# Attention followed by a four-expert layer on one core: a new table of order priorities, and other engines for the last output tiles

## The chip, the cores and the metric

The kernel runs on one core of a Trainium2 chip. The metric is the device time of one execution in microseconds (us), as the median of several runs of the same program. A core has one engine for matrix products (TensorE, PE below), whose weight loads are a row of their own (PEld), VectorE (DVE), ScalarE (ACT), GpSimd (POOL) and SyncE (SP), and 16 DMA engines that move data between the core's own memories and the chip's large one. Each engine runs its own list of instructions in order and waits on semaphores for the others. Products land in PSUM, which here is cut into eight banks of 128 x 512 numbers.

## The reference

Everything is fp32. First there is attention over 8 batches of 8 heads with 64 columns each, 512 local and 32 global positions. Then comes an attention in each of four experts, of which every position takes its best two.

```python
# attention: window = 32, scale = 1/sqrt(64)
s_g   = scale * q_g @ concat(k_g, k_l).T                # global queries see all
out_g = softmax(s_g) @ concat(v_g, v_l)
s_ll  = where(|i - j| <= window, scale * q_l @ k_l.T, -1e9)
s_lg  = scale * q_l @ k_g.T
out_l = softmax(concat(s_lg, s_ll)) @ concat(v_g, v_l)
x     = concat(out_g, out_l)        # turned to (batch, 544, 512)
# experts: 4 of 64 columns each
logits = x @ w_gate                 # top two, softmax over the two -> w
for e in range(4):
    q, k, v = x @ wq[e], x @ wk[e], x @ wv[e]
    a   = softmax(causal(scale * q @ k.T))
    out += w_e * (a @ v @ wo[e])    # only where e is one of the two
```

## The kernel before

**Work.** A pair is two heads of one batch, so there are 32 pairs, four to a batch. For a pair the local attention goes through `p1_load` and `p1_load_values` (loads of kn, qn and of the values v), `p1_trans` (PE turns kn and qn, L575), `p1_scores` (64 small products into two banks, L605), `p1_softmax` (DVE takes scores, mask and minimum out of PSUM, L617; ACT does exp, L620), `p1_ptrans` (PE turns the probabilities, tile st, L638), `p1_av` (64 small products with the values, L668) and `p1_turn` (PE turns the result xn, L638). POOL copies each pair's values into overlapping windows, nine copies a pair (L319: six v<-v, three v<-vg). Global queries have steps of their own (L732, L772). The loads of L335 are all issued by SP, but for the very first.

The experts' part of a batch has the projections `m_v` (L833) and `m_qk` (L802), each a product of high and low parts; the scores `m_scores` (L955, pairs of 512-column banks, two experts c = 0, 1 at a time and three sizes t); `m_softmax` (DVE L970, ACT L974, the normalisation L990 by POOL, or DVE for the last batch); the turn of the probabilities (tile pm, L638, copied out as ptl and ptu by L319 and L317); `m_av` (L1040); the same for the 32 tail positions of a batch (L1062, L1107); and the four output tiles of a batch, with a tail tile for every four batches (`out_tile`: six products L1126, one copy out of PSUM to tile ot, one to four DMAs L1133).

**Order.** The program runs through 42 steps; step s has the scores of pair s, the products with the values of pair s-2, and a quarter of the experts' work of a batch that began six steps before. Nothing is issued in this order, though. Each operation is recorded with an engine (or a choice, as "ACT|DVE"), an expected time in ns, and a priority of 100 times its step plus a small lateness; to this a table adds a number that depends on the operation's kind, its expected time and its step modulo 8:

```python
o.prio += SHIFT.get(kind, {}).get((round(ns[0]), int(self.prio // 100) % 8), 0)
```

One entry so moves all operations of that kind, time and step modulo 8, in all batches. Then `place` puts the operations in a row one at a time, on an assumed clock per engine. For PE it takes the smallest of

```python
f[0] + CHANGE * (f[1].shape != shape) + PULL * (f[1].prio - pe[0].prio)
```

(the time at which it could start, a price where the products divide the PE array otherwise than those before, and a price for low priority); other engines take the lowest priority among what could start soon. Eight PSUM banks, and two to four buffers of each other tile, are given out in the order of the row. So the table decides each engine's list of instructions, and which bank and which buffer is waited for.

**The last tiles.** `out_tile` copies its bank to ot by ACT. The DMA is issued by ACT for tiles 2, 3 and the tail tile, and by SP, as four DMAs, for tiles 0 and 1 (`MIRRORED`). The program ends with the four tiles of batch 7 and the second tail tile.

Of the kernel before, what the change touches and what calls it, by code (L numbers as in the profile page):

```python
# [49 lines left out]
class Op:  # L50
    def __init__(self, k, engs, ns, fn, prio, packets, shape, slow):
# [24 lines left out]
        "evac": {(276, 0): 110, (316, 2): -110, (369, 2): 110, (369, 6): 110, (448, 4): 30, (475, 0): 90, (475, 4):  # L76
        50, (475, 7): 80},
        "high_low": {(477, 3): 140, (477, 5): 100},
        "load": {(540, 1): 80, (540, 4): -150, (540, 7): -150},
        "m_av": {(2220, 1): -60, (2220, 3): -20, (2220, 7): -70},  # L80
        "m_gates": {(130, 7): -30, (350, 7): -110, (630, 6): 150, (648, 3): 150, (950, 7): -150},
        "m_qk": {(1504, 0): -40, (1504, 3): 60, (1504, 4): 40, (1504, 6): -150},
        "m_scores": {(431, 2): 100, (431, 6): 60, (722, 1): -30, (722, 3): 40, (722, 5): 100, (745, 2): -90, (745, 6):
        -20},
        "m_softmax": {(80, 1): -40, (80, 2): 100, (80, 6): -70, (211, 1): 40, (211, 3): 150, (211, 5): -130, (211, 7):
        -40, (386, 1): -150, (386, 7): -150, (431, 7): -50, (477, 1): -120, (477, 3): -100, (492, 4): 100, (492, 6):
        -80, (599, 7): -90, (610, 4): 20, (705, 2): 140},
        "m_tail_av": {(583, 1): -110, (583, 5): 30},
        "m_tail_scores": {(110, 7): -100, (610, 3): 10, (859, 7): -50},
        "m_v": {(1440, 2): -80, (1440, 5): 150},  # L90
        "m_v_tails": {(256, 3): 150},
        "out_tile": {(450, 1): 130, (1400, 1): -70, (1400, 5): 40},
# [12 lines left out]
        "setup": {(163, 2): -70},  # L105
        "turn_halves": {(250, 0): 60, (250, 1): -100, (250, 2): 100, (250, 5): -150, (312, 0): 30, (312, 2): -110,
        (312, 4): 70, (312, 6): -70, (374, 0): -150, (374, 2): -150, (374, 4): -100, (374, 6): 80, (499, 0): 40, (499,
        2): -90, (499, 3): 20, (499, 4): -90, (499, 7): 10},
        "turned": {(84, 1): 10, (84, 3): 50, (84, 5): 50, (84, 7): -70, (255, 5): 150},
}  # L110


class Plan:

    ENGINES = ("PE", "DVE", "ACT", "POOL", "SP")

    def __init__(self):
        self.ops = []  # L120
# [144 lines left out]
def fused_kernel(ctx: ExitStack, tc: tile.TileContext, q_l, k_l, v_l, q_g, k_g, v_g,  # L265
                 w_gate, wq, wk, wv, wo, out):
    nc = tc.nc
    B, H, SL, D = q_l.shape
# [15 lines left out]
    op = plan.op  # L284
# [1045 lines left out]
```

## Time and profile before

| | |
|---|---|
| three runs | 484.69, 485.98, 487.23 us; median 485.98 |
| profiled execution | 484.76 us, span 482.9 us |
| granted PE clock, mean | 0.992 of full speed |
| busy share of the span | PE 95%, PEld 83%, DVE 79%, ACT 67%, POOL 60% |
| instructions | 25126 |

The span runs from the first to the last recorded instruction; 1.9 us of the execution lie outside it. A busy share says how long an engine had an instruction in work, not that it went at its best pace. The profiled execution is 1.2 us below the median of the runs.

### The profile page before, as it was taken

The numbers are of one execution on the slowest core, as the hardware profiler recorded it, in microseconds if no ns is written. First come the engines' busy times: TensorE is split into PE (matmuls) and PEld (weight loads), VectorE is DVE, ScalarE is ACT, GpSimd is POOL, SyncE is SP. The second block draws the span as 40 slices with busy tenths as digits, with TensorE's granted clock in tenths as the row PEclk, the third lists the DMA queues.
The fourth block names the chain that finished last, engine by engine and source line by source line (L and its number), as shares of the span: only waits on it lengthen the run. The fifth ranks groups of instructions, "written<-read, shape, count | busy, mean of one in ns | idle before, by whom it ended". The sixth has DMA issues, their size and how long they took to land.

```text
span 482.9 us, 25126 instructions
## 1 busy us (share of the span) xinstructions
PE 460.3 (95%) x10252; PEld 400.0 (83%) x10252; DVE 380.9 (79%) x1684; ACT 324.4 (67%) x1171; POOL 291.4 (60%) x563
## 2 busy tenths in 40 slices
PE   8869998999999999999999999999999999999987
PEld 6657896888988988879889888879888899789865
DVE  7889589999985986779985977859986786557480
ACT  1867278797865785767955966847885674645472
POOL 8996988978585496809587296916859122311320
PEclk9899999999999999999999999999999999999999
DMA  9967666764355334444256234453022000200123
GB/s 189 199 126 154 123 119 115 150 106 83 67 103 125 68 56 95 111 79 87 41 108 148 50 54 79 104 122 77 3 56 89 4 3 3 70 21 2 27 65 109
DMA packets 182388, 40.96 MB, mean 85 GB/s; under 512 B 177664, under 2 KB 177664, under 8 KB 182272
## 3 DMA queue, kind: packets, MB, share of 16 engines
q1 hardware_dynamic: 172784, 32.96, 35.1%
q10 hardware_dynamic: 9488, 6.40, 4.8%
q8 instruction: 80, 1.31, 1.2%
q14 instruction: 36, 0.29, 0.2%
HBM read 30.42 MB, written 8.91 MB: 81 GB/s over the span
## 4 chain that ended last, share of the span: by engine, by line
PE 77%; DVE 9%; DMA 6%; SPq 2%; issue 2%; POOL 2%; ACT 0%; ACTq 0%; POOLq 0%; DVEq 0%
PE bank L802 15%; PE bank L1126 10%; PE bank L638 9%; PE bank L833 9%; PE bank L1040 7%; PE bank L955 6%; PE bank L605 5%; PE bank L668 5%; PE bank L732 2%; SPq L335 2%; PE bank L772 2%; DMA v<-in_v_l_dram 2%; DMA kn<-in_k_l_dram 2%; PE bank L1062 2%; DVE st L617 1%
## 5 line engine op out<-in xcount | busy, mean ns | idle before, releaser
L319 POOL COPY v<-v 32x512 f32<-32x512 f32 (+3 forms) x192 | 115.8, 604 | 17.8 <-DMA v<-in_v_l_dram 8.2
L990 POOL TENSOR_SCALAR pm<-pm,msm,gate 128x512 f32<-128x512 f32 (+3 forms) x124 | 74.3, 613 | 64.0 <-ACT pm L974 13.3
L620 ACT ACTIVATE st<-st,sm 128x128 f32<-128x128 f32 x256 | 99.6, 393 | 13.0 <-DVE sm L617 12.7
L319 POOL COPY v<-vg 32x640 f32<-32x640 f32 (+1 forms) x96 | 67.2, 702 | 33.5 <-PE bank L772 22.9
L974 ACT ACTIVATE pm<-pm,msm 128x512 f32<-128x512 f32 (+3 forms) x128 | 71.0, 557 | 20.8 <-DVE msm L970 20.7
L617 DVE CUSTOM_DVE_ANT_0 st<-bank,band 128x128 f32<-128x128 f32 x256 | 57.9, 281 | 2.7 <-PE bank L605 2.5
L620 ACT ACTIVATION_READ_ACCUMULATOR st<-st,sm 128x1 f32 x256 | 48.7, 190 | 0.0
L955 PE MATMUL bank<-kt,qt 64*32 64x32 f32 (+15 forms) x1024 | 41.3, 393 | 2.3 <-issue 1.5
L605 PE MATMUL bank<-kd,qp 64*32 64x128 f32 x2048 | 40.1, 276 | 1.4 <-issue 1.1
L317 ACT COPY ptu<-bank 128x384 f32<-128x384 f32 (+1 forms) x42 | 21.4, 543 | 27.6 <-PE bank L638 17.3
L802 PE MATMUL bank<-xh,wk_hi 128*128 128x272 f32 x128 | 38.7, 302 | 0.0
L970 DVE CUSTOM_DVE_ANT_0 pm<-bank,cmask 128x512 f32<-128x512 f32 (+1 forms) x64 | 37.5, 614 | 0.4 <-PE bank L955 0.3
L802 PE MATMUL bank<-xh,wq_hi 128*128 128x272 f32 x128 | 37.3, 292 | 0.0
L833 PE MATMUL bank<-wv_hi,xh 128*128 128x260 f32 x128 | 37.1, 290 | 0.0
L802 PE MATMUL bank<-xl,wk_hi 128*128 128x272 f32 x128 | 36.9, 288 | 0.0
L802 PE MATMUL bank<-xh,wq_lo 128*128 128x272 f32 x128 | 36.9, 289 | 0.0
L802 PE MATMUL bank<-xl,wq_hi 128*128 128x272 f32 x128 | 36.9, 288 | 0.0
L802 PE MATMUL bank<-xh,wk_lo 128*128 128x272 f32 x128 | 36.9, 288 | 0.0
L668 PE MATMUL bank<-v,ptw 128*32 128x64 f32 x2048 | 36.2, 223 | 0.1
L605 PEld LDWEIGHTS bank<-kd,qp 64*32 64x32 f32 x2048 | 32.3, 107 | 4.7 <-issue 2.3
L833 PE MATMUL bank<-wv_lo,xh 128*128 128x260 f32 x128 | 36.3, 283 | 0.0
L833 PE MATMUL bank<-wv_hi,xl 128*128 128x260 f32 x128 | 36.1, 282 | 0.0
(183 smaller groups left out, 1319.7 us busy)
## 6 DMA issues: line engine op xcount, KB each, us to landing
v<-in_v_l_dram SPq DMA_DIRECT2D x61, 120.0 KB, 3.4
kn<-in_k_l_dram SPq DMA_DIRECT2D x104, 64.0 KB, 2.5
qn<-in_q_l_dram SPq DMA_DIRECT2D x104, 64.0 KB, 2.6
out_dram<-ot SPq DMA_DIRECT2D x64, 64.0 KB, 1.7
out_dram<-ot ACTq DMA_DIRECT2D x16, 256.0 KB, 2.8
v<-in_v_l_dram SPq DMA_DIRECT2D x30, 64.0 KB, 3.4
kn<-in_k_l_dram SPq DMA_DIRECT2D x8, 128.0 KB, 3.7
qn<-in_q_l_dram SPq DMA_DIRECT2D x8, 128.0 KB, 4.4
```

Of the source, the lines that this page charges most:

```text
L319: ENG[e].tensor_copy(out, in_)
L605: nc.tensor.matmul(sp[h].t[32 * g:32 * g + 32, 128 * t:128 * t + 128], qp.t[rows, 32 * u:32 * u + 32], kd.t[rows, c:c + 128], start=True, ...
L617: op("DVE", 211, lambda e, h=h, t=t, i=i: nc.vector.tensor_tensor_reduce(out=st.t[:, h, t], in0=sp[h].t[:, 128 * t:128 * t + 128], in1=ban ...
L620: op("ACT", 385, lambda e, h=h, t=t, i=i: nc.scalar.activation(st.t[:, h, t], st.t[:, h, t], AF.Exp, bias=sm.t[:, 0, i:i + 1], scale=-1.0, ...
L638: nc.tensor.transpose(two[y].t[:, k, :], block()[rows], ident[rows, rows])
L668: nc.tensor.matmul(xq.t[32 * g:32 * g + 32, t, h, :], pt.t[:, h, 32 * u:32 * u + 32], v.t[:, h, window(u), :], start=True, stop=True)
L802: nc.tensor.matmul(pp.t, w[:, ch, cols], x(part, ch)[:, n], start=(ch == 0 and w is hi and part == 0), stop=(ch == NCH - 1 and part == 1))
L833: nc.tensor.matmul(pv.t, x(part, ch)[:, 128 * i:128 * i + 128], w[:, ch, :], start=(ch == 0 and part == 0 and w is hi), stop=(ch == NCH - ...
L955: nc.tensor.matmul(sp[x].t[32 * g:32 * g + 32, at:at + n], qt.t[rows, q0:q0 + 32], kt.t[rows, :n], start=True, stop=True)
L974: op("ACT", 280 + 0.83 * n, lambda e, x=x, at=at, n=n, s=s: nc.scalar.activation(pm.t[:, x, at:at + n], pm.t[:, x, at:at + n], AF.Exp, bia ...
L990: lambda e, x=x, at=at, n=n, row=row, s=s: ENG[e].tensor_scalar(pm.t[:, x, at:at + n], pm.t[:, x, at:at + n], sm.t[:, 3, s:s + 1], gate.t[ ...
L1126: nc.tensor.matmul(po.t, lhs(part, c), w[:, c, :], start=(c == 0 and part == 0 and w is hi), stop=(c == 1 and part == 1))
```

## The change

Two things change. The whole table SHIFT has other values, in the same form; the diff shows two lines of each table. And the output tiles of the last batch, with the second tail tile, may have their bank copied by ACT or DVE and their DMAs issued by SP or ACT, whichever `place` finds free, where both were fixed.

```diff
 SHIFT = {
-        "m_av": {(2220, 1): -60, (2220, 3): -20, (2220, 7): -70},
-        "m_qk": {(1504, 0): -40, (1504, 3): 60, (1504, 4): 40, (1504, 6): -150},
...
+        "m_av": {(1560, 1): 110, (2220, 1): 40, (2220, 3): -50},
+        "m_qk": {(1504, 4): 30, (1504, 7): -10},
...
-    def out_tile(y, lhs, dsts, via="ACT"):
+    def out_tile(y, lhs, dsts, via="ACT", last=False):
...
-        evac(lambda: ot.t, lambda: po.t, 512, [po], [ot], "ACT")
+        evac(lambda: ot.t, lambda: po.t, 512, [po], [ot], "ACT|DVE" if last else "ACT")
         for dst, rows in dsts:
-            op(via, 450, lambda e, dst=dst, rows=rows: ENG[e].dma_start(dst, ot.t[rows]), r=[ot], late=-10,
+            op("SP|ACT" if last else via, 450, lambda e, dst=dst, rows=rows: ENG[e].dma_start(dst, ot.t[rows]), r=[ot], late=-10,
...
-        out_tile(y, lambda part, c: M[b, "yo"][part].t[:, c, at:at + 128], dsts, "SP" if i in MIRRORED else "ACT")
+        out_tile(y, lambda part, c: M[b, "yo"][part].t[:, c, at:at + 128], dsts, "SP" if i in MIRRORED else "ACT",
+                 b == B - 1)
...
-                 [(out[4 * g + r, SL:, :], slice(32 * r, 32 * r + 32)) for r in range(4)])
+                 [(out[4 * g + r, SL:, :], slice(32 * r, 32 * r + 32)) for r in range(4)], last=4 * g + 4 == B)
```

The changed file is two lines shorter ahead of its functions, so L335 of before is L333 after, L668 is L666, and so on. Three places show what the table does.

SP's loads at the head of the program, before, from the 13th transfer on. A 128x4x64 tile of kn or qn is the load of one head of pairs 0 to 5 (32x16x32 stands for the later pairs, four a tile), v a piece of a pair's values, in_moe_ the experts' weights.

```order
L335 DMA kn<-in_k_l_dram 128x4x64 x2
L335 DMA qn<-in_q_l_dram 128x4x64 x2
L335 DMA pm<-in_moe_wv_dram 128x8x64 x2
L335 DMA msm<-in_moe_w_gate_dram 128x4x4
L335 DMA pm<-in_moe_wk_dram 128x8x64 x2
L335 DMA v<-in_v_l_dram 96x5x64 x2
L335 DMA v<-in_v_l_dram 128x2x64
L335 DMA v<-in_v_l_dram 96x5x64 x2
L335 DMA v<-in_v_l_dram 128x2x64
L335 DMA kn<-in_k_l_dram 128x4x64
```

The same stretch after:

```order
L333 DMA v<-in_v_l_dram 96x5x64 x2
L333 DMA v<-in_v_l_dram 128x2x64
L333 DMA kn<-in_k_l_dram 128x4x64 x4
L333 DMA qn<-in_q_l_dram 128x4x64 x4
L333 DMA pm<-in_moe_wv_dram 128x8x64 x2
L333 DMA msm<-in_moe_w_gate_dram 128x4x4
L333 DMA pm<-in_moe_wk_dram 128x8x64
L333 DMA pm<-in_moe_wq_dram 128x8x64 x2
L333 DMA pm<-in_moe_wk_dram 128x8x64
L333 DMA v<-in_v_l_dram 96x5x64 x3
L333 DMA vg<-in_v_g_dram 32x8x64
```

Pair 2's values (its first three pieces here) move ahead of the weights, all of kn and qn of the early pairs too, and pair 3's values move behind them: they are the first two of the x3 here and a 128x2x64 piece three transfers on, the 31st, 32nd and 37th of SP, where they were the 25th to the 27th.

PE at the head, before: from the turn of pair 5's kn to the first projection. The two rows of L668 are pairs 2 and 3 with their values.

```order
L575 MATMUL bank_65<-ident,kn 128x128 x4
L668 MATMUL bank_68<-v,ptw 32x64 x32
...
L575 MATMUL bank_69<-ident,qn 128x128 x4
...
L668 MATMUL bank_66<-v,ptw 32x64 x32
L772 MATMUL bank_71<-v,longt 32x64 x20
...
L833 MATMUL bank_68<-wv_hi,xh 128x260
```

After, the same work:

```order
L666 MATMUL bank_64<-v,ptw 32x64 x32
L573 MATMUL bank_67<-ident,kn 128x128 x4
L573 MATMUL bank_66<-ident,qn 128x128 x4
...
L666 MATMUL bank_69<-v,ptw 32x64 x32
L770 MATMUL bank_67<-v,longt 32x64 x20
...
L487 MATMUL bank_66<-ident,ot 128x64 x4
...
L697 MATMUL bank_70<-ident,turned 128x128
L831 MATMUL bank_67<-wv_hi,xh 128x260
```

Pair 2's products with its values no longer stand behind the turn of kn, and two short turns (of batch 1's global queries in ot, and of a product named turned) that followed the first projection now stand ahead of it.

PE near the end, before: the last products of batch 6's output tiles, then the last scores of batch 7.

```order
L1126 MATMUL bank_67<-wo_hi,yl 128x512
L699 MATMUL bank_66<-ident,turned 128x128
L1062 MATMUL bank_64<-kt,qt 32x512 x4
L955 MATMUL bank_69<-kt,qt 32x256
L955 MATMUL bank_65<-kt,qt 32x256
...
L955 MATMUL bank_68<-kt,qt 32x288
L955 MATMUL bank_70<-kt,qt 32x288
```

After:

```order
L953 MATMUL bank_69<-kt,qt 32x160
L953 MATMUL bank_65<-kt,qt 32x160
L1124 MATMUL bank_66<-wo_hi,yh 128x512
...
L1124 MATMUL bank_64<-wo_hi,yl 128x512
L697 MATMUL bank_69<-ident,turned 128x128
...
L1060 MATMUL bank_66<-kt,qt 32x512 x4
L1060 MATMUL bank_68<-kt,qt 32x32 x4
```

All of batch 7's scores but the tail's now stand ahead of batch 6's four output tiles.

## Rows read from the trace of the kernel before

**Rows 1.** Page, part 1: busy us, share of the span, instructions of each engine.

```profile
PE 460.3 (95%) x10252; PEld 400.0 (83%) x10252; DVE 380.9 (79%) x1684; ACT 324.4 (67%) x1171; POOL 291.4 (60%) x563
```

**Rows 2.** Windows: length, busy us (instructions) by engine, PE clock, DMA share, GB/s.

```profile
0.00:20.00 20.00, 16.11 (x250) 12.60 (x257) 15.87 (x71) 9.75 (x40) 16.96 (x53) 0.94 1.05 193
20.00:40.00 20.00, 15.67 (x553) 12.98 (x539) 17.55 (x81) 13.54 (x56) 17.32 (x28) 0.89 0.75 155
40.00:460.00 420.00, 410.59 (x9230) 360.79 (x9234) 337.05 (x1496) 289.50 (x1048) 254.97 (x480) 1.00 0.38 76
460.00:483.00 23.00, 17.93 (x242) 13.68 (x229) 10.39 (x39) 11.61 (x31) 2.16 (x4) 0.98 0.26 83
```

**Rows 3.** Timeline of PE, 30 to 51 us: start, us, instructions [idle before <-releaser].

```profile
30.85 0.34 PE L638 MATMUL bank<-ident,xn 64*128 64x64 f32 x4 [1.35 <-issue]
...
34.89 1.09 PE L575 MATMUL bank<-ident,kn 128*128 128x128 f32 x4 [1.86 <-DMA kn<-in_k_l_dram]
...
39.92 1.38 PE L668 MATMUL bank<-v,ptw 128*32 128x64 f32 x64
41.61 0.77 PE L772 MATMUL bank<-v,longt 128*32 128x64 f32 x40 [0.32 <-DVE longt L319]
...
44.91 0.27 PE L638 MATMUL bank<-ident,st 64*128 64x64 f32 x2 [0.54 <-ACT xh L328]
...
46.47 0.38 PE L833 MATMUL bank<-wv_hi,xh 128*128 128x260 f32 x1
...
50.84 0.34 PE L489 MATMUL bank<-ident,ot 64*128 64x64 f32 x2 [0.59 <-DMA ot<-in_q_g_dram]
```

**Rows 4.** Timeline of SP's queue, 14 to 32 us.

```profile
14.71 0.94 SPq L335 DMA_DIRECT2D kn<-in_k_l_dram  x2
...
27.37 4.05 SPq L335 DMA_DIRECT2D kn<-in_k_l_dram  x6
```

**Rows 5.** Page, part 6: DMA issues, KB each, median us from issue to landing.

```profile
v<-in_v_l_dram SPq DMA_DIRECT2D x61, 120.0 KB, 3.4
```

**Rows 6.** Timeline of POOL, 45 to 60 us.

```profile
45.17 7.58 POOL L319 COPY v<-v 32x640 f32<-32x640 f32 x12
...
56.43 3.80 POOL L319 COPY v<-v 32x640 f32<-32x640 f32 x6
```

**Rows 7.** Timeline of PE, at 211 and at 281 us.

```profile
211.43 0.62 PE L955 MATMUL bank<-kt,qt 64*32 64x256 f32 x16 [0.44 <-issue]
...
281.82 0.77 PE L638 MATMUL bank<-ident,pm 64*128 64x64 f32 x18 [0.24 <-POOL pm L990]
```

**Rows 8.** Timeline of DVE, at 210 us.

```profile
210.24 0.69 DVE L970 CUSTOM_DVE_ANT_0 pm<-bank,cmask 128x512 f32<-128x512 f32 x1 [0.33 <-PE bank L955]
...
211.47 0.28 DVE L617 CUSTOM_DVE_ANT_0 st<-bank,band 128x128 f32<-128x128 f32 x1
```

**Rows 9.** Timeline of PE, 461 to 469 us.

```profile
461.50 0.96 PE L638 MATMUL bank<-ident,pm 64*128 64x64 f32 x24
...
467.41 1.56 PE L638 MATMUL bank<-ident,pm 64*128 64x64 f32 x24
```

**Rows 10.** Chain of waits, from 455 us: start, us, what.

```profile
462.13 0.33 DVE ptu L319
...
469.78 2.38 PE bank L1040 x24
472.16 7.20 PE bank L1126 x30
...
479.39 0.58 ACT ot L317
```

**Rows 11.** Groups by line and form, L319 and L317: duration ns min/median/max.

```profile
L319 DVE COPY ptw<-bank x24: 633/680/692, 17.4 to 406.2; 128x512 f32<-128x512 f32 x24
```

**Rows 12.** The same of L317, on ACT.

```profile
L317 ACT COPY ot<-bank x34: 561/580/588, 143.4 to 479.4; 128x512 f32<-128x512 f32 x34
```

**Rows 13.** Page, part 5: a group, out<-in xcount | busy, mean ns | idle before.

```profile
L605 PE MATMUL bank<-kd,qp 64*32 64x128 f32 x2048 | 40.1, 276 | 1.4 <-issue 1.1
```

More of the change, by code (lines that the diff above doesn't have):

```diff
@@ L75 @@
 SHIFT = {
[L76 to L79, printed above, removed]
-        "m_av": {(2220, 1): -60, (2220, 3): -20, (2220, 7): -70},
-        "m_gates": {(130, 7): -30, (350, 7): -110, (630, 6): 150, (648, 3): 150, (950, 7): -150},
-        "m_qk": {(1504, 0): -40, (1504, 3): 60, (1504, 4): 40, (1504, 6): -150},
@@ L83 @@
[L83 to L89, printed above, removed]
@@ L90 @@
-        "m_v": {(1440, 2): -80, (1440, 5): 150},
-        "m_v_tails": {(256, 3): 150},
-        "out_tile": {(450, 1): 130, (1400, 1): -70, (1400, 5): 40},
[12 rows of a table removed]
[L105 to L109, printed above, removed]
+        "evac": {(180, 2): -80, (262, 2): 50, (316, 2): -90, (316, 4): -90, (369, 4): -150, (475, 0): -80, (475, 2):
@@ new lines @@
+        70, (475, 3): 30},
+        "high_low": {(332, 2): 150, (477, 7): 150, (598, 1): -120},
+        "load": {(540, 2): 150, (540, 4): 150},
+        "m_av": {(1560, 1): 110, (2220, 1): 40, (2220, 3): -50},
+        "m_qk": {(1504, 4): 30, (1504, 7): -10},
+        "m_scores": {(431, 0): 30, (431, 2): 120, (431, 6): 40, (722, 7): -70, (745, 0): -120, (745, 2): 80},
+        "m_softmax": {(80, 4): 80, (211, 3): 100, (211, 7): -20, (386, 1): 130, (386, 3): 80, (599, 1): 150, (610, 0):
+        -10, (610, 4): -100},
@@ new lines @@
+        "m_tail_av": {(583, 5): -90},
+        "m_tail_scores": {(100, 7): 130, (110, 3): -40, (610, 7): -100, (859, 7): -10},
+        "m_v": {(1440, 2): -60, (1440, 6): 30},
+        "m_v_tails": {(256, 3): 140, (330, 3): 80},
+        "out_tile": {(1400, 5): 20},
[12 rows of a table added]
+        "setup": {(1000, 1): 150, (1000, 2): 100},
+        "turn_halves": {(250, 1): 60, (250, 3): 50, (250, 6): -20, (312, 0): 150, (312, 2): -130, (312, 6): 60, (374,
+        0): 20, (374, 4): -120, (499, 1): 60, (499, 3): 60, (499, 4): -30, (499, 5): -130, (499, 6): 20, (499, 7):
@@ L110 @@
+        -70},
+        "turned": {(84, 3): -10, (84, 5): 130, (220, 5): -60, (222, 5): 150, (222, 7): -150, (255, 3): 60, (255, 7):
+        100},
 }
```

24 rows, old and new, of the table SHIFT are left out of this document.

## The prediction

> **What bounds the kernel now.** First the busy shares: PE 460.3 of 482.9 us, DVE 380.9, ACT 324.4, POOL 291.4 [rows 1]. The reader is to see that no other engine comes near PE, and that the change gives PE exactly the same products: only an order can be won, at most PE's 22.6 us without an instruction, plus what is hidden in stretched products. Then the windows, to see where these 22.6 us lie [rows 2]: 3.9 us in the first 20, 4.3 in the next 20, 9.4 in the 420 us between 40 and 460, 5.1 after 460. The middle is so full (98%) that a new order has little to take there and can spoil more. The head and the tail are thinner, so these are read step by step. In the head, the timeline of PE shows four waits [rows 3]: 1.35 us before the turn of xn at 30.85, 1.86 us at 34.89 for the load of pair 5's kn, 0.32 us at 41.61 and 0.54 us at 44.91; pair 3's products with the values (L668) start at 39.92 and the first projection (L833) at 46.47. In the tail, the chain of waits runs from 462.13 to 469.78 through DVE (scores, normalisation and copies of the last probabilities, 7.65 us), then through the last m_av, 7.2 us of output tiles and ACT's last copy [rows 10].
>
> **The change part by part.** The sum is made against the profiled execution, 484.76 us (span 482.9, so 1.9 us outside it, left as they are). It is 1.22 us below the median of the runs, 485.98, and that is added at the end.
>
> *(a) Head, to the first projection.* What is moved: pair 2's values come before the weights, pair 5's kn and qn too, and pair 3's values come behind them. Pair 5's kn, which PE waits for at 34.89, was SP's 33rd transfer and is about the 19th, and in PE's order pair 2's products no longer stand behind its turn, so the 1.86 us go. What is late next is pair 3's values. Their place on SP is worked out in bytes. Before, from 14.71 to 27.37 us [rows 4] SP issued four tiles of kn and qn (128 KB each, from the shapes in the order), four halves of weights (256 KB each), the gate's 8 KB, four 120 KB and two 64 KB pieces of values: 2152 KB in 12.66 us, 170 KB a us. After, ahead of pair 3's first piece there are three pieces of pair 2 (304 KB), eight tiles of kn and qn (1024), six halves of weights and the gate (1544): 2872 KB, 16.9 us, so that piece is issued at about 31.6 and the second, for the other head, 0.7 us later, at 32.3. A 120 KB piece lands 3.4 us after its issue [rows 5]: 35.7. The third piece, six transfers and 608 KB behind the first, is issued 3.6 us after it and lands at 38.6. POOL spreads a pair in six copies, 3.80 us [rows 6]: 35.7 + 3.8 = 39.5, the third piece being there by then. So pair 3's products start at 39.5 instead of 39.92. From there to the first projection before took 6.55 us [rows 3], of which 0.32 and 0.54 were waits: 5.7 us of work, 45.2 instead of 46.47, that is 1.3 us earlier. And two short turns that stood behind the first projection are now ahead of it, some 0.4 us of work (the one of ot is 0.34 us [rows 3]). (a) is -1.7 us. Bounds: no wait left at all, -(1.35 + 1.86 + 0.32 + 0.54) - 0.4 = -4.5; or POOL has another pair's copies ahead of pair 3's, 3.80 us more [rows 6], so that its products start at 43.3 and the projection at 49.0, less the 0.4: +2.1.
>
> *(b) The next stretch.* PE waits 0.59 us at 50.84 for the load of batch 1's q_g into ot [rows 3]. Its transfer was SP's 57th or 58th and is the 38th or 39th, so the wait goes: -0.5. Bounds -0.9 (a little gained elsewhere by earlier loads) and +0.6 (the same wait for another tile).
>
> *(c) The middle, to 460 us.* Two things move here. First, scores come in longer runs. Counted through PE's order, runs of scores without other products between them that fill nine banks or more were six (9, 9, 9, 10, 12 and 12 banks) and are nine (three each of 9, 11 and 12). There are eight banks, so in such a run PE must wait until DVE has taken out the first scores. DVE takes 0.62 us for a bank of experts' scores (210.24 to 211.47 is two of them [rows 8]); PE's wait in the run at 211.43 was 0.44 us [rows 7]. Against these the runs before had the same waits, only in fewer places. Second, waits for POOL's normalisation, as the 0.24 us at 281.82 [rows 7], fall where probabilities are turned later. The rows price neither in the new order. The sum of both has as its lower bound half of the 9.4 us without an instruction, -4.7, since the other half is spread over some ten kinds of waits of which an order removes one and makes another; the upper bound is nine runs that each cost one more pair of evictions less the wait there already is, 9 x (1.24 - 0.44) = +7.2. I take -0.5, near zero, because nothing in the rows says that either prevails.
>
> *(d) Tail.* The chain through DVE from 462.13 to 469.78 [rows 10] begins when the last scores are in. All of batch 7's scores but its tail's now stand ahead of batch 6's four output tiles, some 5.7 us of PE's work (four of the five tiles that take 7.2 us [rows 10]) in which DVE, 45% busy after 460 us [rows 2], can do its part. Before, PE had 5.07 us without an instruction after 460, of which 3.6 lie after its last product at 479.36 (479.39 less the gap to ACT's copy), so 1.4 of waits; and 24 turns of pm took 1.56 us at 467.41 where the same took 0.96 at 461.50 [rows 9], 0.6 of waits in small pieces. That is 2.0 us in all. I take -1.2: the tail's scores, its softmax and its turn are still behind the output tiles. Bounds -2.0 and +0.5 (one copy of 0.58 us late).
>
> *(e) The last copies.* ACT copied five tiles, each 0.58 us in 1.4 us of PE's products (7.2 / 5), so moving some to DVE frees nothing. Two stay with ACT, three go to DVE, the last among them: DVE took 0.68 us for such a copy [rows 11], ACT 0.58 [rows 12]: +0.1. The last DMA is one of 256 KB from ACT's queue in both orders. Who issues the earlier DMAs: 0, since 1.4 us or more of products follow each of them; without that cover a late copy would add its 0.58 us.
>
> *(f) Array shapes.* The changes from products that divide the array one way to products that divide it another fall from 170 to 165. A change can cost no more than the time one product stays in the array, 276 ns by the mean of the scores [rows 13]: at most 1.4 us for five, and as little as nothing, as products overlap. Counted 0, inside the range.
>
> One rule bears on (c) and (f). The Trainium skill, "TensorEngine Tiling (Array Packing)", section "Performance Considerations" (PSUM Bottleneck), says that cutting the array into tiles makes TensorE faster but not the emptying of PSUM, which may then become the limit; its "Key Properties" say that a change of the mode drains TensorE. By the first, longer runs of scores speak against this change; that is the third rival below, and the 0.44 us in the run at 211.43 agrees with it. By the second, (f) is a gain, of a size that the page does not give.
>
> Sum: -1.7 - 0.5 - 0.5 - 1.2 + 0.1 = -3.8, 484.76 to 481.0 us; with the 1.22 us to the median, **482.2 us**.
>
> **The rivals.** *The middle gains too.* If the new order also removes half of the idle time between 40 and 460, (c) is -4.7 instead of -0.5: 482.2 - 4.2 = 478.0. For it: these waits are all of the kind that an order makes (a bank, a turn, a normalisation). Against it: 98% is already much. *The runs eat it.* If only the three additional long runs cost a pair of evictions each, 3 x 1.24 = 3.7 us, (c) is +3.7 and the time 482.2 + 4.2 = 486.4, no change. For it: the wait at 211.43. Against: DVE has 19.7% of the middle free (337.05 of 420 us [rows 2]). *The other side: all nine runs wait for DVE.* If DVE is behind when each begins, as it is where copies of turned probabilities stand ahead, each costs 0.8 us more: (c) is +7.2 and the time 482.2 + 7.7 = 489.9. It decides from 0.63 us a run, where (c) is +5.7 and the time passes 488.4. For it: 80% busy DVE and longer runs; against: the runs of before, as long as these, sit in a middle of 98%. *The change does nothing* is no case apart: all engines' orders differ, and it ends with the second.
>
> **How the numbers follow.** The forecast case has a chance of 0.45 and its own range, 480 to 484.5: (a), (b) and (d) reach their bounds together rarely, so it takes about half of the way to each (2.2 us below, 2.3 us above). The middle's gain has 0.20, the runs that eat it 0.22, the other side 0.13. Within 0.5%, 2.4 us, of 485.98 is about what a measurement of this kernel cannot tell from no change, so faster means below 483.55 and slower above 488.4. Faster: 0.40 of the first case and 0.20, together 0.60; same: 0.22, the upper edge of the first case (0.05) and 0.01 of the other side, 0.28; slower 0.12. The range leaves out the other side and the far end of the gain: 477.3 to 487.0.
>
> **What would show it.** (a) right: pair 3's products with the values start near 39.5 and the first projection near 45.2, no wait for kn ahead of pair 2's products; wrong if pair 3's start later than 40. (b): no wait for ot near 50 us. (c): PE's time without an instruction between 40 and 460 stays within 1 us of the 9.4; the rivals show in waits for a bank in the middle of a run of scores, or in their absence. (d): the last chain goes through PE, not DVE, between the last scores and the last m_av, and 1 us less lies between the first of batch 6's output tiles and the end. (e): the last copy is DVE's, 0.68 us. The prediction is wrong if the middle moves by more than 2 us either way, as no row of before prices it.

## The result and the profile after

The changed kernel takes 479.87 us (median of 4 runs, 476.46 to 481.32) against 485.43 us before (4 runs): a ratio of 0.987, 95% interval 0.983 to 0.991, faster by 1.3%. A second measurement of its order gave 0.9868 (0.9842 to 0.9894; after_again below). The profiled execution took 476.46 us, span 474.7 us, against 484.76 and 482.9. The lines of the changed kernel's source are two lower than before: the products with the values, L668 before, are L666.

The page of the changed kernel, part 1, columns as in [rows 1]:

```profile
PE 453.9 (96%) x10252; PEld 398.2 (84%) x10252; DVE 382.7 (81%) x1688; ACT 323.2 (68%) x1166; POOL 292.0 (62%) x564
```

Its windows, columns as in [rows 2]:

```profile
0.00:20.00 20.00, 15.71 (x302) 11.88 (x302) 15.96 (x76) 9.15 (x37) 16.93 (x53) 1.00 1.05 190
20.00:40.00 20.00, 14.59 (x522) 11.59 (x525) 19.14 (x78) 17.41 (x65) 17.30 (x27) 1.00 0.79 169
40.00:460.00 420.00, 413.16 (x9349) 366.95 (x9337) 342.93 (x1525) 293.10 (x1058) 257.74 (x486) 1.00 0.38 77
...
```

The same 10252 products take 6.4 us less of PE's busy time, and PE is without an instruction for 20.8 us instead of 22.6. In the first 40 us this time has grown, from 8.2 to 9.7 us; between 40 and 460 it has fallen from 9.4 to 6.8. So the head, for which the largest gain was forecast, gained nothing, and the middle gained most. Four points in PE's timeline divide the two spans:

| stretch | before | after | of it forecast |
|---|---|---|---|
| start to the first projection | 46.47 | 46.43 | -1.3 |
| to the first product of batch 6's output tiles | 407.0 | 402.3 | -0.4 -0.5 -0.5 |
| to PE's last product | 25.9 | 22.3 | -1.2 |
| to the span's end | 3.60 | 3.69 | +0.1 |

(The -1.7 of (a) are -1.3 to the first projection and -0.4 behind it, for two turns that now stand ahead of it.)

The third row is not like for like. In the new order 48 scores and 24 turns of pm of batch 7 have moved from it into the second, and 8 scores of the tail the other way. From each product's start to the next one's, these 48 scores took 1.65 us before, 24 turns take 0.9 and 8 scores of the tail 0.5, so some 2.0 us of work have changed rows. Of the scores 40 stand in this line of before:

```profile
460.28 1.29 PE L955 MATMUL bank<-kt,qt 64*32 64x256 f32 x40
```

The turns stand here after:

```profile
445.66 0.96 PE L636 MATMUL bank<-ident,pm 64*128 64x64 f32 x24
```

So the tail gained 1.5 us and the middle 6.8 us in these two profiles. One profile of each is not enough to size this: over the experiments below, the second row is 405.5 to 407.1 in four profiles with the late part in the old order (before, head_new, early_new, swap; mean 406.5) and 402.3 to 406.1 in six with it new (after, after_again, late_new, rest_new, values_first, route_old; mean 404.3), a gain of 4.2 us when the 2.0 us are counted. It is uncertain by some 1.5 us: after and route_old, which have the same order up to the last tiles, are 3.8 us apart. With the tail's 1.5 that makes 5.7 us, and the medians are 5.6 apart.

*The head.* PE's timeline of the changed kernel, 36 to 47 us (answers to [rows 3]):

```profile
36.41 0.30 PE L666 MATMUL bank<-v,ptw 128*32 128x64 f32 x4
37.79 0.30 PE L666 MATMUL bank<-v,ptw 128*32 128x64 f32 x2 [1.07 <-POOL v L317]
39.47 1.02 PE L666 MATMUL bank<-v,ptw 128*32 128x64 f32 x57 [1.38 <-POOL v L317]
...
44.14 0.28 PE L636 MATMUL bank<-ident,xn 64*128 64x64 f32 x2 [0.52 <-issue]
44.70 0.41 PE L487 MATMUL bank<-ident,ot 64*128 64x64 f32 x4
46.10 0.33 PE L697 MATMUL bank<-ident,turned 128*128 128x128 f32 x1 [0.63 <-DVE xl L327]
46.43 0.39 PE L831 MATMUL bank<-wv_hi,xh 128*128 128x260 f32 x1
```

Pair 3's first six products stand at 36.41 and 37.79, with a wait for POOL's spreading of the values behind each group (1.07 and 1.38 us); 57 of the 64 stand at 39.47, where the forecast had all of them from 39.5 on. Two more waits, 0.52 and 0.63 us, stand ahead of the first projection. POOL itself was held up by the load, as its timeline shows (12 copies are two pairs'; pair 3's six lasted until 39.42):

```profile
34.33 8.96 POOL L317 COPY v<-v 32x640 f32<-32x640 f32 x12 [1.45 <-DMA v<-in_v_l_dram]
```

The forecast had the first projection at 45.2. The turn of ot, which waited 0.59 us for its load before, stands at 44.70 and waits for nothing.

*The middle.* The waits of PE by line and releaser, in the stretch from 47 us to the last scores (us in total, times, longest). Before, 47 to 453 us:

```profile
PE bank L955 <- issue: 1.5, 3, 0.7
PE bank L605 <- issue: 1.1, 3, 0.5
PE bank L638 <- POOL pm L990: 1.0, 4, 0.3
PE bank L638 <- DVE xl L329: 0.8, 3, 0.4
PE bank L489 <- DMA ot<-in_q_g_dram: 0.6, 1, 0.6
PE bank L638 <- ACT longt L317: 0.6, 1, 0.6
PE bank L955 <- DVE ptw L319: 0.5, 1, 0.5
...
```

After, 47 to 448 us, all rows:

```profile
PE bank L666 <- issue: 1.8, 1, 1.8
PE bank L730 <- issue: 1.0, 2, 0.8
PE bank L603 <- issue: 0.8, 1, 0.8
PE bank L1038 <- ACT ptw L315: 0.7, 2, 0.3
PE bank L953 <- issue: 0.4, 1, 0.4
PE bank L636 <- issue: 0.3, 1, 0.3
PE bank L636 <- DVE msm L968: 0.2, 1, 0.2
```

Waits for another engine or a load were 4.5 us and are 0.9; waits that the profile can put down to nobody ("issue") were 3.5 us and are 4.3. (Waits of 0.15 us or less are not listed.) Over the whole stretch the new order so took away waits of turns and scores for POOL, DVE and ACT (L638, L955). How much of the gain that is, the cut at 112 us tells (below, "Where in the middle").

*The tail.* The end of the chain of waits of the changed kernel, answering to [rows 10]: start, us, what.

```profile
448.76 5.79 PE bank L1124 x24
...
455.30 1.05 PE bank L1060 x16
456.36 2.34 PE bank L1038 x24
...
458.72 1.36 ACT ptu L315 x3
460.08 0.39 ACT ptl L315
...
460.52 0.87 PE bank L1038 x8
...
464.00 6.99 PE bank L1124 x30
...
471.07 0.69 DVE ot L317
```

Before, the chain ran 7.65 us through DVE. Now it lies on PE through batch 6's output tiles, as forecast, and leaves it once ahead of the last copy, for 1.8 us of ACT's copies of turned probabilities, in which PE waits 0.63 us.

### The profile page after: what moved, and what is told of

Its sections match the earlier page's. It is cut to its first block, busy times and chain, and to the rows that moved or that the text cites. A ratio compares the mean times of both kernels' runs of the same rounds, so it can differ in the third digit from the quotient of the medians.

```text
span 474.7 us, 25116 instructions
## 1 busy us (share of the span) xinstructions
PE 453.9 (96%) x10252; PEld 398.2 (84%) x10252; DVE 382.7 (81%) x1688; ACT 323.2 (68%) x1166; POOL 292.0 (62%) x564
## 3 DMA queue, kind: packets, MB, share of 16 engines
q1 hardware_dynamic: 172688, 32.83, 35.7%
q8 instruction: 80, 1.31, 1.2%
## 4 chain that ended last, share of the span: by engine, by line
PE 83%; DVE 5%; DMA 3%; POOL 2%; issue 2%; SPq 2%; ACT 1%; ACTq 0%; DVEq 0%; POOLq 0%
PE bank L800 18%; PE bank L636 10%; PE bank L1124 10%; PE bank L831 10%; PE bank L1038 8%; PE bank L953 6%; PE bank L603 6%; PE bank L666 5%; PE bank L730 3%; PE bank L770 2%; SPq L333 2%; POOL v L317 2%; DMA kn<-in_k_l_dram 2%; PE bank L1060 1%; DMA qn<-in_q_l_dram 1%
## 5 line engine op out<-in xcount | busy, mean ns | idle before, releaser
L988 POOL TENSOR_SCALAR pm<-pm,msm,gate 128x512 f32<-128x512 f32 (+3 forms) x125 | 76.1, 624 | 96.2 <-ACT pm L972 30.1
L317 POOL COPY v<-v 32x512 f32<-32x512 f32 (+3 forms) x192 | 115.7, 602 | 25.1 <-DMA v<-in_v_l_dram 15.4
L317 POOL COPY v<-vg 32x640 f32<-32x640 f32 (+1 forms) x96 | 65.1, 680 | 10.7 <-PE bank L770 5.6
L603 PE MATMUL bank<-kd,qp 64*32 64x128 f32 x2048 | 41.9, 273 | 2.4 <-issue 2.1
L666 PE MATMUL bank<-v,ptw 128*32 128x64 f32 x2048 | 37.2, 220 | 5.6 <-POOL v L317 3.0
L953 PE MATMUL bank<-kt,qt 64*32 64x352 f32 (+14 forms) x1024 | 42.1, 394 | 0.4 <-issue 0.4
L666 PEld LDWEIGHTS bank<-v,ptw 128*32 128x32 f32 x2048 | 31.4, 110 | 9.9 <-issue 4.5
```

The costliest lines, as they stand in the source:

```text
L317: ENG[e].tensor_copy(out, in_)
L603: nc.tensor.matmul(sp[h].t[32 * g:32 * g + 32, 128 * t:128 * t + 128], qp.t[rows, 32 * u:32 * u + 32], kd.t[rows, c:c + 128], start=True, ...
L666: nc.tensor.matmul(xq.t[32 * g:32 * g + 32, t, h, :], pt.t[:, h, 32 * u:32 * u + 32], v.t[:, h, window(u), :], start=True, stop=True)
L953: nc.tensor.matmul(sp[x].t[32 * g:32 * g + 32, at:at + n], qt.t[rows, q0:q0 + 32], kt.t[rows, :n], start=True, stop=True)
L988: lambda e, x=x, at=at, n=n, row=row, s=s: ENG[e].tensor_scalar(pm.t[:, x, at:at + n], pm.t[:, x, at:at + n], sm.t[:, 3, s:s + 1], gate.t[ ...
```

## The experiments

For these the search in `place()` was replaced by a written list of operations with their engines, so that an order can be kept, cut and edited:

```diff
-            best = None
-            for e in self.ENGINES:
...
-            t, e, o = best
+            e, o = ORDER[len(self.ops) - left]
+            o = self.ops[o]
```

With the list of the old order and of the new one, BEFORE and AFTER below, this gives the two kernels' own orders. Ratios are to the kernel before on the same chip, whose medians there were 485.32 (the first four runs), 487.29 (the next four) and 486.78 (the last four).

**The head alone, and all but the head.** In head_new the new order holds up to the first projection, in rest_new from there on.

```diff
+ORDER = AFTER[:363] + [x for x in BEFORE if x not in AFTER[:363]]     head_new
+ORDER = BEFORE[:357] + [x for x in AFTER if x not in BEFORE[:357]]    rest_new
```

> All operations that the changed kernel's order has ahead of its first projection stand in that order; everything behind stands in the order of before. Theory 1 (the middle holds the gain): first projection at about 46.4 us as in both profiles, with some 0.7 us of small turns done earlier, so -0.5 to -1 against before. Theory 2 (the head decides, since PE's clock dips there in the profile of before at 16 to 24 and 32 to 40 us and not in the profile after): -3 to -5, with a clock of 1.00.

> The other half of that pair: the order of before up to its first projection, the changed kernel's order behind it. Theory 1: -4.5 to -6 against before (middle -4.8 and tail -1.8 by the two profiles, less what the seam costs). Theory 2: -1 to -2.5, with the clock dips of before in the first 40 us.

head_new gave 485.43 us, 1.0003 (0.9977 to 1.0029): the head is worth nothing. rest_new gave 484.78 us, 0.9987 (0.9969 to 1.0004), although the tail and the middle are new. PE's timeline shows a seam: the turn of ot, which the new order has early, waits for a load that now stands late on SP.

```profile
52.17 0.66 PE L487 MATMUL bank<-ident,ot 64*128 64x64 f32 x4 [4.83 <-DMA ot<-in_q_g_dram]
```

So the time of rest_new tells nothing of the sum, but it prices term (b) when it goes wrong: one small turn whose load is issued too late costs 4.83 us in front of the whole middle.

**The tail alone, and the new order again.**

```diff
+ORDER = BEFORE[:3160] + [x for x in AFTER if x not in BEFORE[:3160]]  tail_new
+ORDER = AFTER                                                        after_again
```

> The order of before up to some 430 us (all that stands ahead of batch 7's second pair of experts' scores, sizes 0 and 2), the changed kernel's order behind it, with its engines for the last copies and DMAs. Theory 1: -1.2 to -1.8, as the tail's chain goes through PE and no longer through DVE between the last scores and the last m_av. Rival (the tail's gain needs the order that came before it, whose buffers and engines it found free): 0 to -0.5, with new waits for ACT or DVE ahead of m_av.

> The order of the changed kernel, word for word, taken from a written list instead of from the table; nothing else differs. Theory 1 (the gain lies at places in the order, most of it in the middle): a median of 479 to 481 us, -5 to -6 against before. Theory 2 (the profiled execution of the changed kernel, 476.46 us, was fast by chance, since it alone had a granted clock of 1.00 from end to end): times spread from 476 to 481.5, and those with a lower clock are the longer ones; where the clock is below 1.00, it is in the first 45 us, and the middle from 40 to 440 us has PE waits of 23 to 24 us as before (28.5 in the kernel before).

tail_new gave 484.57 us, 0.9976 (0.9953 to 0.9998), and its last stretch, from batch 6's first output product to PE's last product, took 22.3 us as in the changed kernel. (The row ahead of it, in which its seam lies, was long in its profile: 411.8 us, 2.0 of it moved work.) after_again gave 479.28 us, 0.9868. With the head at nothing and the tail at 0.24%, most of the 1.3% has to come from between them.

**Where in the middle.** A cut at 112 us, both ways.

```diff
+ORDER = AFTER[:952] + [x for x in BEFORE if x not in AFTER[:952]]     early_new
+ORDER = BEFORE[:940] + [x for x in AFTER if x not in BEFORE[:940]]    late_new
```

> The other half: the changed kernel's order up to 112 us, the order of before behind it, its last copies and DMAs as before. Theory 1: 0 to -1 against before. Rival: -4 to -6, with a clock near 1.00 over the first 50 us.

> The order of before up to 112 us (no PE operation stands in other company at this seam), the changed kernel's order behind it. The seam of rest_new is gone, where a turn of ot waited 4.83 us for a load that the other order had placed late. Theory 1 (the gain is in the middle from 112 us on and in the tail): -5 to -6.5 against before, median 479 to 480.5, PE waits from 120 to 440 us 13.5 to 15.5 (18.4 in the kernel before). Rival (the gain is before 112 us, by the clock or the loads): -0.5 to -1.5.

early_new gave 487.25 us, 1.0002 (0.9966 to 1.0038); late_new 480.97 us, 0.9857 (0.9823 to 0.9891). All of the gain lies behind 112 us. early_new shows why waits alone don't give the time: between 47 and 450 us its waits for other engines are 1.5 us instead of 4.5, but its waits for nobody are 6.2 us instead of 3.5, and the stretch takes 407.1 us, as before.

The two parts can be read apart at PE's 2717th product, at 119 us before and 118 after, ahead of which all orders have done the same work. From the first projection to there, waits for other engines are 1.7 to 2.9 us in the old order (before, head_new, swap, late_new) and 0.0 to 0.2 in the new (after, after_again, early_new), but waits for nobody are none in the old and 2.7 to 3.2 in the new, and the time is the same, 71.4 to 72.8 and 71.5 to 72.0 us. There the waits for engines went and gave nothing. Behind that product, where the gain lies, PE's waits before, 119 to 453 us:

```profile
PE bank L955 <- issue: 1.5, 3, 0.7
PE bank L605 <- issue: 1.1, 3, 0.5
PE bank L638 <- POOL pm L990: 1.0, 4, 0.3
PE bank L1040 <- issue: 0.4, 1, 0.4
...
```

After, 118 to 448 us, all rows:

```profile
PE bank L730 <- issue: 1.0, 2, 0.8
PE bank L1038 <- ACT ptw L315: 0.7, 2, 0.3
```

Means over the four profiles with the late part in the old order and the six with it new, to batch 6's output tiles:

| | old | new |
|---|---|---|
| length | 334.5 (333.6 to 335.2) | 331.9 (330.3 to 333.6) |
| waits for another engine or a load | 1.6 | 0.7 |
| waits for nobody | 3.4 (3.1 to 3.7) | 2.0 (1.0 to 3.4) |

With the 2.0 us of moved work the gain here is 4.6 us. Waits for engines are 0.9 of it and waits for nobody 1.4; half of it is in no wait.

**Is it the length of the runs of scores, or what stands ahead of them?** The second and third rivals hang on PE's 0.44 us in a run of scores at 211.43 us [rows 7], which I had read as a wait for a bank. In the old order, at that run and at the one at 322 us, the first products with the values (L668) were moved ahead of the turn of st (L638), so that the copies which hold the banks can begin sooner.

```diff
 L638 MATMUL bank_70<-ident,long 128x64
-L638 MATMUL bank_65<-ident,st 128x64
...
-L668 MATMUL bank_71<-v,ptw 32x64 x32
+L668 MATMUL bank_65<-v,ptw 32x64 x32
+L638 MATMUL bank_69<-ident,st 128x64
...
 L955 MATMUL bank_66<-kt,qt 32x416
```

> The order of before with one edit at two places (207.4 and 319.3 us of its profile): a pair's products with its values go ahead of the turn of the next pair's probabilities, which stood directly ahead of them. That turn's copies go to the single buffer ptw, which the products still read, so before they began 1.07 us after the turn's end and held two banks while a run of scores began. Theory A (in a run of scores PE waits for banks that copies hold, and so for what stands ahead of the run): the copies of ptw start with the turn's end, PE's waits in these two runs (1.06 and 1.32 us in all) fall below 0.4 each, -1 to -2 us against before. Theory B (it waits for DVE, by the length of the run): the waits stay at 1.0 to 1.3 us, 0 us.

In swap PE's wait in the first run did not go:

```profile
210.64 0.62 PE L955 MATMUL bank<-kt,qt 64*32 64x256 f32 x16 [0.56 <-issue]
```

At the second place, where before had waited 0.70 us, the same products stand at 322.90 and wait for nothing. Both runs have kept their length, so the length does not decide. What stands ahead is not cleanly told by this edit either (what decides is shown with the instruction transfers below): at the first place ACT's copies of the turned probabilities still began only at 208.20 us, when the run had begun at 208.10. The changed kernel says more on the length. Its run at 207 us fills 11 banks and PE's timeline has no wait in it:

```profile
208.56 1.72 PE L953 MATMUL bank<-kt,qt 64*32 64x480 f32 x34
...
211.40 0.87 PE L1038 MATMUL bank<-ptl,vt 128*64 128x256 f32 x8
```

The median of swap, 485.21 us, 0.9958 (0.9932 to 0.9984), is some 2 us lower than before, of which its profile shows only 0.6 in the stretch that it changes (406.4 instead of 407.0 us). The rest I can't explain.

**Does POOL hold the head?** In the new order pair 3's value loads were moved ahead of the halves of wk and wq on SP.

```diff
 L333 DMA msm<-in_moe_w_gate_dram 128x4x4
+L333 DMA v<-in_v_l_dram 96x5x64 x2
+L333 DMA v<-in_v_l_dram 128x2x64
 L333 DMA pm<-in_moe_wk_dram 128x8x64
...
-L333 DMA v<-in_v_l_dram 96x5x64 x3
+L333 DMA v<-in_v_l_dram 96x5x64
```

> The order of the changed kernel with one edit: SP issues pair 3's three pieces of values ahead of three halves of weights (wk and wq, 256 KB each) instead of behind them. In the profile of the changed kernel pair 3's products waited 1.07 and 1.38 us for POOL's copies of these values, which began at 34.33 after 1.45 us of waiting for the load. Theory A (the load decides): POOL starts at about 32.9, the first projection starts 1.4 us sooner or a little more, -1 to -2 against the changed kernel. Theory B (POOL's 12 copies of 8.96 us decide, or the next wait takes the place): 0 to -0.5 against the changed kernel.

It gave 480.75 us, 0.9861 (0.9823 to 0.9898), the same as the change. POOL began at 33.21 instead of 34.33 us, and the wait for it went, but PE's timeline has the next one in its place:

```profile
38.51 0.27 PE L636 MATMUL bank<-ident,long 64*128 64x64 f32 x1 [1.91 <-ACT long L737]
...
39.84 1.93 PE L666 MATMUL bank<-v,ptw 128*32 128x64 f32 x64
```

Pair 3's products now all start at 39.84. Behind POOL stands ACT: in the head two or three engines are late by about the same time, and taking one of them out gives nothing.

**What is the wait for nobody?** A theory formed on these traces: PE waits for its own instructions. The page's part 3 has 80 transfers of a queue of its own in both kernels (this row is of the kernel after):

```profile
q8 instruction: 80, 1.31, 1.2%
```

1.31 MB in 80 transfers is 16 KB each. PE has 20504 weight loads and products, 256 for each transfer, 64 bytes each. One by one in the traces of before and after these transfers take 0.9 to 1.6 us, and many of the waits for nobody end 1.2 to 1.5 us behind the end of one: at 211.43 before, the transfer began at 208.67 and took 1.38; at 323.65, 321.23 and 0.93. The theory says that the waits sit at places counted in instructions; the rival, that they sit where the order makes PE wait for something. To tell them apart, small products were added in front of everything (work is added, nothing is left out; what they write is overwritten), which shifts the whole count:

```diff
+            for i in range(64):
+                nc.tensor.matmul(some[0].t[:32, 64 * (i % 8):64 * (i % 8) + 64], zero.t.bitcast(F32)[:, :32], zero.t.bitcast(F32)[:, :64], start=True, stop=True)
```

> The order of before, unchanged, with 64 more tiny products (and their 64 weight loads, so 128 instructions of PE) at the very start, where PE waits for the first loads anyway; their result is in a bank that is overwritten. Theory F (PE waits for its own instructions: in the traces so far PE resumes from 16 to 22 of its waits 1.2 to 1.6 us after one of the 16 KB transfers of queue 8, which carry instructions, 80 in the program, so 256 instructions each): every such boundary falls 128 instructions earlier in the program, so the waits ahead of the scores L955 in the runs at 209 and 321 us (0.82 and 1.08 us from one weight load to the next) are gone from there, and waits of this kind stand at other places; their sum over 40 to 440 us, 8.2 us in before, may go either way by 3 us; the median within 3 us of before. Theory B (banks that DVE or ACT still hold): the waits stand at the same products as before, 0.7 to 1.1 us each.

> The same 128 instructions ahead of the changed kernel's order. Theory F: its waits of this kind (5.2 to 8.7 us over 40 to 440 us in two profiles) move to other products; the gain against before, -5.5 to -6, changes by up to 3 us either way. Rival (the gain is in what the engines wait for from each other, and the instructions are a constant tax): 478.5 to 481 us as without them.

The edit missed its aim: each of these float32 products is two in the trace, each with its own weight load, so 64 of them are 256 instructions, a whole transfer (81 are counted), and the count is the same again behind them. shift_before gave 489.87 us, 1.0066 (1.0042 to 1.0091), and its wait in the run of scores stands at the same product as before, 6.8 us later in the trace:

```profile
218.19 0.62 PE L953 MATMUL bank<-kt,qt 64*32 64x256 f32 x16 [0.70 <-issue]
```

shift_after gave 485.57 us, 0.9974 (0.9948 to 1.0001), 4.3 us less than shift_before: with the count again in the old place, the change is worth this much. Both times hold the added products, 7.8 to 8.4 us at the start, where PE waited in part anyway. Half as many, 128 instructions, is the shift that was wanted, with the same order of everything else:

```diff
-            for i in range(64):
+            for i in range(32):
```

> The same with 32 products, 64 instructions. As for shift_after; if the times of the three positions (0, 64, 128) differ by over 2 us, the position of the boundaries is worth as much as a third of the change's gain; if they lie within 1 us, it is worth nothing in sum.

shift32_after gave 488.59 us, 1.0035 (1.0009 to 1.0061): with half of the added work, 3.0 us more than shift_after. The waits of PE in shift_after, 46 to 456 us, in which four rows of waits for nobody make 6.2 us:

```profile
PE bank L664 <- issue: 3.1, 4, 2.0
PE bank L601 <- issue: 1.6, 2, 1.1
PE bank L728 <- issue: 1.2, 2, 1.0
...
```

And in shift32_after, 46 to 458 us, all rows:

```profile
PE bank L664 <- issue: 6.5, 7, 1.6
PE bank L601 <- issue: 4.5, 5, 1.5
PE bank L634 <- DVE longt L315: 0.5, 1, 0.5
PE bank L1103 <- issue: 0.3, 1, 0.3
```

The waits for nobody have gone to other products and grown to 11.3 us. Of the waits of 0.3 us or more in that stretch, whoever they are put down to, these have an instruction transfer whose end lies 1.1 to 1.6 us before PE goes on:

```
                before   after   shift_after   shift32_after
waits           12       6       9             14
behind one      7        4       5             12
```

(For before and after the stretch is that from 47 us to the last scores.) By chance such a window of 0.5 us behind 81 transfers in 487 us would catch about one wait in twelve.

All fourteen traces together settle it. Between 40 and 470 us they have 114 waits for nobody of 0.2 us or more, and each of them ends 1.2 to 1.7 us after the end of an instruction transfer. Of the 119 waits of that size put down to an engine or a load, 11 do, about what chance gives. And counted among PE's weight loads and products by their starts (the first is 0), they stand at fixed places, whatever the product there: the wait at 211.43 before is at number 9617; swap and tail_new wait at 9617 too, head_new at 9619, and shift_before at 9873, which is 9617 + 256. shift_after and shift32_after both wait at 8847 and at 10887, one at products of L664 and the other at products of L601. In swap the wait at the second place is gone because the transfer ended in time, at 321.61, 1.29 us before that product (number 14721 in both) could start.

So the theory stands. The waits for other engines did not come back with the shift. But the place of the transfers is part of what the change won: behind the 2717th product waits for nobody fell from 3.4 to 2.0 us, and with the transfers half a step off, the new order has 11.3 us of them in all and takes 3.0 us more than with a whole step, at half of the added work. A half-step shift of the old order was not run, so it is open how much of the gain would be left if both orders were read at many places. It is a cost that lies under every order, and each order falls with its small products on other transfers.

**The last copies.** In the new order, the last copies and DMAs with the engines of before (entries of the list, in words):

```diff
-("DVE", copy of a last tile) x3, ("SP" or "ACT", its DMA)
+("ACT", copy of a last tile) x3, (the queue of before, its DMA)
```

> The changed kernel's order with the last tiles' copies and DMAs given back to the engines that had them before (copies ACT; DMAs SP for tiles 0 and 1, ACT otherwise). If the forecast's step (e) is right: -0.1 us against the changed kernel (the last copy takes 0.58 us on ACT, 0.69 on DVE), not measurable, 0.984 to 0.991 of before. Rival (ACT's copies queue up behind each other or behind DMA issues at the end): +0.5 to +1.

It gave 483.26 us, 0.9923 (0.9894 to 0.9951), 2.4 us of it behind PE's last product: 6.08 us to the span's end instead of 3.69. That is the edit's doing. In its list ACT's copy of the third tile stands ahead of the first two, and ACT's timeline shows the last two copies waiting for a DMA to empty their buffer:

```profile
474.40 1.07 ACT L315 COPY ot<-bank 128x512 f32<-128x512 f32 x2 [3.73 <-PE bank L1124]
...
478.59 0.59 ACT L315 COPY ot<-bank 128x512 f32<-128x512 f32 x1 [2.62 <-DMA out_dram<-ot]
...
479.75 0.59 ACT L315 COPY ot<-bank 128x512 f32<-128x512 f32 x1 [0.58 <-DMA out_dram<-ot]
```

So it does not price the choice of engines alone; for that there is only the profile of the change (below, (e)).

## Why the prediction was right and wrong

The time, 479.87 us, lies in the range, and 2.3 us below the 482.2 forecast, just outside the forecast case's own range (480 to 484.5). That the sum came near is in part luck: (a) and (b) gave 2.2 us that no run shows, and (c) was too small by some 3.7. By its own test, that it is wrong if the middle moves by more than 2 us, its account of where the gain comes from was wrong: the middle moved by about 4, and PE's time without an instruction there by 2.6 us (9.4 to 6.8), not by less than 1.

*(a) Head, forecast -1.7, measured 0.* The step that failed is "of which 0.32 and 0.54 were waits: 5.7 us of work": I took the waits behind pair 3's products as gone with nothing in their place. 0.52 and 0.63 us of new ones came, and values_first showed the next behind these (ACT, 1.91 us). head_new and early_new both give nothing for this part. The 39.5 us for pair 3's products was met by two errors that cancel: POOL began at 34.33 and not at 35.7, and its six copies took 5.1 us and not 3.80. The 0.7 us of turns that now stand ahead of the projection didn't show in the time either. And the 1.35 us at 30.85, which the lower bound took as a wait that can go, ends 1.43 us behind an instruction transfer.

*(b) The load of ot, forecast -0.5.* The wait is gone, as forecast. That it gave time is not shown apart from the rest: early_new has it and gained nothing.

*(c) Middle, forecast -0.5, measured about -4.* The step that failed is the size, set near zero "because nothing in the rows says that either prevails". 98% busy was no proof that waits which go must come back elsewhere, and the rival in which the middle gains too (-4.7, 478.0 us, chance 0.20) was nearer than the forecast. Of the mechanisms named, waits for POOL, DVE and ACT did go, but behind the 2717th product, where the gain lies, they are only 0.9 us of it. The sum had nothing for PE's waits for its own instructions (1.4 us fewer there), and nothing for products that run closer together: counted over the trace from each product's start to the next one's, the 128 tail scores (L1062) take 8.1 us before and 6.3 after, and 6.1 to 6.5 us in every run with the late part new; in the new order they lie among other scores. That these three make the gain is argued from the traces and not tested one by one.

*The two rivals against it* fell with one reading. The 0.44 us in the run at 211.43 was no wait for a bank but for PE's own instructions: it ends 1.38 us behind an instruction transfer, it stays at its number in swap and, 256 further on, at its product in the whole-transfer shift, and the 11-bank run after has no wait. So a pair of evictions per long run, 1.24 us, was the price of something that did not happen. The Trainium skill, "TensorEngine Tiling (Array Packing)", section "Performance Considerations", says that emptying PSUM may become the limit when the array is tiled; as the limit the traces here don't show it: PE's waits for the copies of ptw and ptu out of PSUM are 1.0 us between 47 us and the last scores before and 0.7 after, with DVE 82% busy (342.93 of 420 us) between 40 and 460 us.

*(d) Tail, forecast -1.2, measured -1.5* in the stretch when the moved work is counted, and by time alone 0.24% in tail_new, 1.2 us with an interval up to 2.3. The step was right (the chain goes through PE and not DVE between the last scores and the last m_av), and its size agrees. Of the 0.8 us left for the tail's own softmax and turn, 0.63 us is there, as PE's wait for ACT's copy.

*(e) The last copies, forecast +0.1, measured +0.09*: DVE's last copy took 0.69 us where ACT's took 0.58 [rows 11, 12], and the stretch behind PE's last product 3.69 instead of 3.60.

*(f) Array shapes, forecast 0:* no run here tells five changes of shape from none.

## What to carry to other kernels

Read the waits of the full stretch by releaser before saying that it has nothing to give, and then read them again where an experiment has put the gain: here nearly all waits for other engines went, but those of the first 118 us were replaced by waits for instructions and gave nothing. Waits for nobody move with every order, and one small shift can nearly double them, so compare two orders at more than one place of the count. A head in which several engines are late by the same time gives nothing for an earlier load; look for what is second before counting the first. And a wait put down to "issue" is not a wait for a buffer until an edit of that buffer moves it: count the instructions ahead of it, change that count, and see whether it moves.

## What the runs showed of the hardware

PE waits for its own instructions: 80 transfers of 16 KB, 256 instructions each, 0.9 to 1.6 us, and PE going on 1.2 to 1.7 us after the end of one, in all 114 waits for nobody of 0.2 us or more between 40 and 470 us of fourteen traces. The products of the first attention stage are small (64 with the values in 1.38 us, which with their weight loads is half a transfer [rows 3]), and it is there that the long waits lie: 1.8 us at once in the kernel after at 68.50 us, 1.6 and 1.5 us in shift32_after. In the new order a shift of the count by half a transfer costs 5 us of such waits (6.2 to 11.3 us), about as much as the whole change won.

The granted clock of the profile before was 0.71 at 16 to 20 us and 0.73 at 36 to 40 us, that is the lower level (1.2 GHz) for part of it; it fell at 17.7 and at 34.8 us, when PE had waited 0.86 and 1.86 us for loads. In the profile after it was 1.00 throughout, though PE waited for loads and engines there too, so what made it fall is not shown. Of six runs of after_again three had a mean clock of 0.996 to 0.999 and took 477.40 to 478.86 us, three had 0.988 and took 479.71 to 480.71 us. So some 2 us of the 8.3 us between the two profiled executions may be the clock's and not the change's. Between orders the mean clock tells nothing: rest_new had 0.978 to 0.989 and the time of before.
